# Causal block attention and a mixer block: one written order of 1,507 operations replaced by another

## The chip, the core and the metric

The kernel runs on one core of a Trainium2 chip. The metric is the device time of one execution in microseconds (us), as the median over runs. The core has five engines that work side by side, each through a queue of its own, in order: TensorE (PE; its weight loads are listed apart as PEld), VectorE (DVE), ScalarE (ACT), GpSimd (POOL) and SyncE (SP). POOL's and SP's words here are for the most part issues of DMA transfers. TensorE writes to PSUM, which is cut into banks of 128 x 512 fp32; DVE and ACT read results out of it.

## What is computed

Attention in 8 batches of 8 heads, 576 positions of 64 elements, with a mask of blocks of 64 (a query sees the keys of its own block and of those before it), then a mixer block of two layers on the heads joined to 512 channels:

```python
def _attn_ref(q, k, v):
    B, H, S, D = q.shape                       # 8, 8, 576, 64
    scores = 1.0 / np.sqrt(D) * np.matmul(q, k.transpose(0, 1, 3, 2))
    scores = np.where(block_i >= block_j, scores, -1000000000.0)   # blocks of 64
    attn = np.exp(scores - np.max(scores, axis=-1, keepdims=True))
    attn = attn / (np.sum(attn, axis=-1, keepdims=True) + 1e-09)
    return np.matmul(attn, v).astype(np.float32)

def _moe_ref(x, w_tok1, w_tok2, w_ch1, w_ch2):  # x: heads joined, 8 x 576 x 512
    h = np.maximum(x.transpose(0, 2, 1) @ w_tok1, 0.0) @ w_tok2    # 256 wide
    u = x + h.transpose(0, 2, 1)
    return u + np.maximum(u @ w_ch1, 0.0) @ w_ch2                  # 1536 wide
```

## The kernel before

The program is a list of operations, made once when the kernel is built. Each operation (`P.add`) names the engines that may do it, the operations it depends on, the PSUM banks that it takes and gives back, and a function that emits its instructions. There are 1,509 of them, numbered in the order in which they were added. Their order in time is not worked out when the kernel is built: it is written out in the string `ORDER` (lines 97 to 175), and `Plan.placed` walks it. A word of `ORDER` is a number, an engine letter (T TensorE, A ScalarE, D VectorE, P GpSimd, S SyncE) and, for operations that take PSUM, the letters of the banks: a to d are the four `mm` banks, s and t the two score pairs of the first attention (`sc`), e to h the `late` banks, which stand in the place of s and t once batch 0's scores are done. Each engine's queue holds its own words in that order, and what an operation depends on becomes a wait on a semaphore ahead of it. `ORDER` thus also fixes which engine evacuates a bank and which bank it is.

What runs, stage by stage:

- *Start.* SyncE loads k of the first four heads of batch 0 as fp32 in two halves of 288 KB: rows 0 to 8 are word 13S, rows 9 to 17 word 16S (L426). ScalarE casts them to bf16 (14A and 17A, L395). POOL loads q of those heads in three parts (19P 144 KB, 21P 80 KB, 23P 64 KB, L437), then V (L471), the other heads' k and q, and batch 1's. VectorE transposes each part (15D and 18D for k, 20D, 22D and 24D for q, L442).
- *First attention* (`first_attention`). Score sets (`score_set`, L569) of two heads or four go to the score pairs, and an exponential (`exp`, L587, 128x1024) reads each; there are two pairs, so a third set waits for the first exponential. `tail` copies and clears an edge of the exponentials (L595, L600) on VectorE or POOL. `head_out` (L617) and `ends_out` (L670) multiply with V; a reciprocal and a product on VectorE (L637, L643) make rows of x.
- *Warming matmuls* (`raise_clock`). They multiply zeros: one operation (43) of `WARM` = 11 matmuls of 512 columns (L366) and up to `KEEP` = 37 operations of one matmul of 256 columns (L373; numbers from 44 on). A KEEP word may be left out of `ORDER`; 35 are in it.
- *Later batches.* `attention` makes scores for a batch in six sets of four heads (L569), with exponentials of 128x512 (L776); `token_mix` does the token layer (`token_up` L811 and L815; for batch 0 `first_u`, L871, whose transposes wait for an add on VectorE; u at L910 and L925); `channel_up` (L1038) and its later forms do the first channel layer, `first_down` (L1460) and `channel_down_fast` (L1369, folds at L1393) the second. Where `channel_down_fast` is used, sums and differences of weights and activations stand in for part of the products. The stages of neighbouring batches are woven into each other, so that TensorE has products of one batch while another waits for exponentials.
- *V of the later batches.* `load_v` has five loads per batch (351 to 355 for batch 2; 525 to 529 for batch 3). A load into the buffer of an earlier batch waits for that batch's head outputs.

TensorE works in different tiles of its array: score sets use 32 rows, head outputs and the layers all 128, the row sums of odd pairs another cut. Going from one to another is called a change of tile here.

Of the kernel before, what the change touches and what calls it, by code (L numbers as in the profile page):

```python
# [27 lines left out]
class Plan:  # L28
# [89 lines left out]
    419D 531A 440Tb 97D 414Tc 534A 325Te 533A 98D 326T 532A 415D 437A 416D 542Tahgf 99D 441A 438Tc 545A 327T 439D
    544A 444D 463Tgd 543A 445D 448Thb 328D 466A 464Tc 451D 546A 329S 411Ta 408Te 465A 446D 469T 412D 690P 413D 449Tf
    523D 470A 454T 529P 450A 409D 442Ta 410D 452Tc 455A 443D 691P 467Tg 520D 453A 537Taefh 447D 692P 468A 456T 521D  # L120
    538A 473T 689P 524D 539A 471T 679D 540A 683P 596Ta 457D 541A 474D 562Tcefh 597A 678D 458T 566A 681D 594Ta 565A
    459D 564A 460D 476T 563A 595D 461T 477A 569Tchfe 682D 462A 472D 604Ta 847P 571A 478Tdb 475D 686P 572A 605D 602Tg
    535P 481A 600Th 603D 536P 570A 598Ta 567P 482Tf 601D 607S 568P 553Tc 844P 599D 483A 479Tg 550Th 554D 555D 480A
    488T 551D 484T 552D 606S 489D 486T 485A 556Tc 487D 491T 573A 574Thadg 557D 490D 492A 547Te 558D 577A 493D 497Tbf
    575A 548D 576A 549D 559Tc 578A 688D 701Tedah 498A 685D 579Tg 560D 704A 684D 499T 705A 494D 850P 702A 693P 580D
    585Ta 703A 581D 503T 500D 687D 706Tgdbh 586D 587D 561D 591Te 504D 710A 501Ta 709A 495D 708A 592D 707A 593D 582Tc
    502D 627Tbd 612The 608D 630A 588Tg 583D 496D 505T 859P 615D 858P 633T 584D 506D 507T 857P 634A 589D 590D 860P
    694Tcgab 508D 856P 618T 698A 849D 509T 697A 846D 696A 619D 695A 760Tb 609D 610D 699P 510D 738Tacgh 761A 848D
    631Tf 742A 611D 942P 628Tb 741A 632D 758Th 700P 740A 853P 629D 739A 845D 635T 759A 726Tcbag 636D 723Th 730A 637T
    724D 729A 725D 717Tf 638D 762Th 727A 764Ta 728A 718D 719D 640T 763D 731P 733Tfcbg 641A 732P 765D 768Th 737A 851D  # L130
    766Td 772S 735A 720Ta 769D 711Tg 736A 746Tc 721D 722D 734A 616Th 767D 714Ta 617A 613Tb 712D 773S 713D 642Tdf
    747D 614A 748D 620T 715D 645A 716D 743Tg 622T 621D 639A 648T 744D 511S 745D 646Tb 854D 512S 649A 861Tcagh 338S
    647A 623D 643Td 863A 624D 652T 862A 644D 752Ta 865A 650T 653D 625T 864A 753D 749Tc 754D 626A 655T 866P 852D
    868Tadhg 867P 651D 656A 755Te 871A 770Tf 775D 952P 869A 654D 794Tbh 756D 750D 872A 751D 951P 795Ta 776D 797A
    779Tgc 757D 939P 796D 870A 780Te 782A 800T 657D 798Ta 781A 855D 783Td 771A 785T 799A 784D 948P 809Tef 801A 953P
    802T 777D 812A 778D 787T 803D 945P 786A 804T 815T 788D 789T 805D 816A 905Tbadg 790D 813Te 908A 807T 906A 814D
    792T 808A 810Td 658D 907A 817T 909A 811D 661Tbh 793A 818D 873Tadcg 662D 819T 875A 943D 667T 876A 820D 877A 944D
    874A 822T 941D 893Tdceg 821D 823A 887Ta 659D 897A 884Tf 663T 894A 888D 889D 895A 885D 886D 896A 940D 900Tadcg
    898P 664D 890Tf 904A 899P 881Te 949D 1037P 903A 925Tb 882D 955P 883D 902A 891D 892D 901A 878Te 947D 1040P
    968Tfcdg 926A 950D 954P 922Ta 969A 879D 665Tb 880D 1046P 971A 946D 970A 923D 924D 1043P 972A 956Tedfa 666D 913Tc  # L140
    668D 959A 916Tg 914D 669T 958A 915D 917D 957A 918D 660D 960A 910Td 919Tc 961D 995Tgafe 911D 1052P 920D 921D 670D
    999A 927Tc 1053P 998A 912D 962D 997A 791D 1050P 963Tdbef 996A 671T 928A 1042D 967A 1041D 966A 1000Tacgf 965A
    672D 979Te 964A 1039D 976Tb 1003A 673T 980D 977D 1004A 981D 978D 1002A 988Tbedg 1001A 674D 973Tc 991A 1047D
    1022Tf 676S 990A 974D 975D 989A 1038D 982Ta 992A 985Tc 806D 1054Tdbhe 983D 1023A 984D 993P 1020Tg 1044D 994P
# [1439 lines left out]
```

## Time and profile before

| | us |
|---|---|
| median of 3 runs | 284.48 |
| lowest, highest | 284.04, 285.65 |
| span of the profiled execution | 284.7 |
| TensorE busy | 275.8 |
| VectorE busy | 240.3 |
| ScalarE busy | 180.4 |
| POOL busy | 71.7 |

The profiled execution is one of its own beside the three timed runs; its span, from its first instruction to its last, is what its records give, and no other time of it is known. The views shown below are: the page's busy times and its 40 slices of 7.1 us; busy time of each engine within stretches of the span; the chain of waits, that is, the work that ended last, followed back in time, with start, length, and engine or line; the timeline, with start, length, engine, line, operation, output and input; and the landings of DMA transfers. "issue" in the chain is time in which the engine waited for nothing that the profile shows. Line numbers are those of the kernel before.

### The profile page before, as it was taken

The page shows a single profiled execution, that of the slowest core. Times are in us where ns is not written, and L with a number is a line of the kernel's source. Part 1 is how long each engine was busy: PE and PEld are TensorE (multiplying, and loading weights), DVE is VectorE, ACT ScalarE, POOL GpSimd, SP SyncE. Part 2 cuts the span into 40 slices and gives each one's busy share as a digit, 9 for nine tenths or more (in the row PEclk, how much of TensorE's full clock was granted, in tenths as well). Part 3 has the DMA queues.
Part 4 walks back from the last instruction along what each step waited for, and adds up shares of the span by engine and source line. Part 5 has one row for each costly group of instructions (what it writes and reads, how often), then busy time and mean ns, then how long its engine had stood idle before and what let it go on. Part 6 is the DMA issues. An engine that isn't in the chain of part 4 may idle for free.

```text
span 284.7 us, 9438 instructions
## 1 busy us (share of the span) xinstructions
PE 275.8 (97%) x4038; PEld 197.6 (69%) x4038; DVE 240.3 (84%) x519; ACT 180.4 (63%) x325; POOL 71.7 (25%) x120
## 2 busy tenths in 40 slices
PE   7998999999999899999999999999999999999994
PEld 3667656556878676987777658744488876468883
DVE  3589569799999799999998997997998987598893
ACT  3798685778888358996879785136546653764000
POOL 8975635170641062060341220000000000000000
PEclk9999999999999999999999999999999999999999
DMA  8999999969989495898199587130033403000246
GB/s 160 166 174 202 190 205 203 137 94 134 144 120 119 71 84 87 225 135 122 11 169 102 87 106 132 49 119 18 2 74 98 126 7 131 12 2 0 104 127 212
DMA packets 64776, 31.79 MB, mean 112 GB/s; under 512 B 53088, under 2 KB 55904, under 8 KB 64736
## 3 DMA queue, kind: packets, MB, share of 16 engines
q0 software_dynamic: 45040, 17.64, 53.1%
q1 hardware_dynamic: 19696, 13.57, 19.6%
q8 instruction: 31, 0.51, 0.7%
q14 instruction: 9, 0.07, 0.1%
HBM read 35.85 MB, written 9.44 MB: 159 GB/s over the span
## 4 chain that ended last, share of the span: by engine, by line
PE 92%; DVE 2%; ACT 2%; DMA 1%; issue 1%; SPq 0%; DVEq 0%
PE late L1369 14%; PE mm L1369 11%; PE late L1235 7%; PE mm L1111 7%; PE late L1111 6%; PE mm L569 6%; PE mm L1235 6%; PE mm L617 4%; PE mm L811 3%; PE mm L910 3%; PE mm L1038 3%; PE late L569 2%; PE late L617 2%; PE late L811 2%; PE mm L1460 2%; PE late L1460 2%
## 5 line engine op out<-in xcount | busy, mean ns | idle before, releaser
L776 ACT ACTIVATE e_sb<-late 128x512 bf16<-128x512 f32 x89 | 50.5, 609 | 10.4 <-PE late L569 9.1
L776 ACT ACTIVATE e_sb<-mm 128x512 bf16<-128x512 f32 x79 | 45.1, 609 | 9.9 <-PE late L569 6.6
L471 POOL DMA_DIRECT2D vals<-in_v_dram x45 | 37.2, 844 | 26.7 <-PE late L617 15.9
L442 DVE STREAM_TRANSPOSE qk_sb<-qk_sb 128x288 int32<-128x288 int32 (+2 forms) x57 | 36.2, 694 | 4.6 <-ACT qk_sb L395 3.5
L1369 PEld LDWEIGHTS <-sums 128*128 128x128 bf16 x288 | 27.6, 98 | 5.6 <-issue 1.8
L1369 PEld LDWEIGHTS <-gT 128*128 128x128 bf16 x288 | 27.8, 98 | 4.6
L569 PEld LDWEIGHTS <-qk_sb 32*64 32x64 bf16 x1280 | 19.9, 104 | 13.1 <-issue 8.8
L569 PE MATMUL mm<-qk_sb 32*64 32x64 bf16 (+7 forms) x546 | 27.8, 291 | 0.0
L569 PE MATMUL late<-qk_sb 32*64 32x512 bf16 (+7 forms) x594 | 27.1, 291 | 0.0
L617 PEld LDWEIGHTS <-e_sb 128*128 128x128 bf16 x640 | 23.8, 97 | 4.1 <-issue 0.9
L1111 PEld LDWEIGHTS <-ws_sb 128*128 128x128 bf16 x192 | 17.8, 98 | 3.4 <-issue 1.3
L797 ACT ACTIVATE gT<-mm 128x512 bf16<-128x512 f32 x25 | 14.7, 601 | 7.8 <-PE mm L1111 3.0
L617 PE MATMUL mm<-vals,e_sb 128*128 128x65 bf16 x430 | 19.0, 193 | 0.0
L643 DVE TENSOR_TENSOR x_sb<-mm,rinv 128x256 bf16<-128x256 f32 x43 | 17.9, 421 | 1.1
L1111 PEld LDWEIGHTS <-wc_sb 128*128 128x128 bf16 x144 | 15.4, 114 | 1.8 <-issue 0.2
L1235 PEld LDWEIGHTS <-ws_sb 128*128 128x128 bf16 x96 | 9.3, 98 | 10.1 <-issue 0.2
L1369 PE MATMUL late<-wd_sb,sums 128*128 128x256 bf16 x108 | 13.6, 272 | 1.2 <-issue 1.2
L1369 PE MATMUL late<-wd_sb,gT 128*128 128x256 bf16 x120 | 14.7, 273 | 0.0
L595 POOL COPY vals<-e_sb 128x256 bf16<-128x256 bf16 x10 | 4.1, 412 | 40.9 <-issue 22.9
L395 ACT COPY mm<-late 128x512 f32<-128x512 f32 x17 | 9.9, 584 | 7.1 <-PE late L1235 5.0
L797 ACT ACTIVATE gT<-late 128x512 bf16<-128x512 f32 x17 | 10.2, 602 | 6.3 <-PE late L1235 3.4
L1235 PE MATMUL late<-e_sb,ws_sb 128*128 128x512 bf16 x44 | 12.6, 379 | 0.0
(203 smaller groups left out, 656.2 us busy)
## 6 DMA issues: line engine op xcount, KB each, us to landing
out_dram<-o_sb SPq DMA_DIRECT2D x14, 512.0 KB, 3.1
vals<-in_v_dram POOLq DMA_DIRECT2D x28, 128.0 KB, 5.4
qk_sb<-in_k_dram POOLq DMA_DIRECT2D x12, 288.0 KB, 6.3
qk_sb<-in_q_dram POOLq DMA_DIRECT2D x12, 288.0 KB, 5.9
out_dram<-o_sb SPq DMA_DIRECT2D x7, 256.0 KB, 3.2
wc_sb<-in_moe_w_ch_dram POOLq DMA_DIRECT2D x8, 192.0 KB, 7.7
wc_sb<-in_moe_w_ch_dram POOLq DMA_DIRECT2D x3, 512.0 KB, 10.4
vals<-in_v_dram POOLq DMA_DIRECT2D x15, 64.0 KB, 4.9
```

The costliest lines, as they stand in the source:

```text
L442: nc.vector.transpose(dst[:, 0:S, :] .rearrange("p s e -> p (s e)") .bitcast(I32) .rearrange("p (a k) -> p k a", k=NB)[:, k0:k1], raw2.bit ...
L471: nc.gpsimd.dma_start(out=t[128 - p : 128, J, hs, 0:64], in_=src)
L569: nc.tensor.matmul(out=home(n)[64 * half : 64 * half + 64, c : c + w], lhsT=bar[r, 0] if j is None else kT[i][r, 64 * j : 64 * j + 64, par ...
L617: nc.tensor.matmul(out=u[:, I, 0:65], lhsT=e[:, h, c : c + 128], rhs=vt[:, J, head, 0:65], start=(J == 0), stop=(J == I),)
L643: nc.vector.tensor_tensor(out=xt[:, 0:4, 64 * head : 64 * head + 64], in0=u[:, :, 0:64], in1=ri[:, 0:4].to_broadcast([128, 4, 64]), op=MULT,)
L776: nc.scalar.activation(dst, bank_of(x), EXP, scale=scale)
L797: nc.scalar.activation(dst, src, RELU)
L811: nc.tensor.matmul(out=ps, lhsT=w1_sb[:, c, tt : tt + 255 : 2], rhs=xt[:, c, cols], start=(c == 0), stop=False)
L1111: nc.tensor.matmul(out=bank_of(bank)[:, 256 * o_ : 256 * o_ + 256], lhsT=x(o_, m), rhs=y[:, :, m, :], start=opens, stop=m == 1, skip_group ...
L1235: nc.tensor.matmul(out=bank_of(bank), lhsT=x(m), rhs=y[:, :, m, :], start=first and m == 0, stop=m == 1, skip_group_check=not first,)
L1369: nc.tensor.matmul(out=bank_of(bank)[:, 256 * i : 256 * i + 256], lhsT=x[:, kk, 128 * i : 128 * i + 128], rhs=y[:, kk], start=first and i ...
L1460: nc.tensor.matmul(out=ps, lhsT=gT[0][:, cc, 128 * si : 128 * si + 128], rhs=wc2_sb[:, cc, :], start=cc == 0, stop=cc == NDC - 1,)
```

## The change

Only the string `ORDER` is replaced. It has 76 lines instead of 77, so that every line behind it is numbered one lower in the changed kernel (the score sets are L568 there, head outputs L616). Of the 1,509 operations the old string places 1,507 and the new one 1,485: 22 of the words of KEEP are gone, and 13 are left. All other operations are the same.

What differs beside those: on SyncE 13S goes ahead of 16S. On POOL q's loads are in the order 19P, 21P, 23P instead of 21P, 19P, 23P, and V's loads stand elsewhere. On VectorE the first transposes are 20D, 15D, 22D, 24D, 18D instead of 15D, 20D, 22D, 18D, 24D. TensorE's first score set is 100 instead of 125, and from there on nearly every word has another place. Some evacuations are done by another engine (VectorE's words go from 519 to 522, ScalarE's from 324 to 323, POOL's from 115 to 118, SyncE's from 40 to 35), and five of the last batch's output stores are issued from ScalarE's queue instead of SyncE's. Bank letters differ throughout.

```diff
 ORDER = """
-    16S 0A 11D 10D 13S 9D 21P 1D 2D 43Ta 5D 19P 4D 3D 23P 33P 27P 14A 25P 31P 15D 29P 17A 20D 37P 44Tb 45Tb 46Tb 22D
-    47Ta 36P 48Ta 49Ta 18D 50Ta 51Ta 52Ta 35P 53Ta 24D 54Ta 55Ta 56Ta 125Ts 34P 100Ttbc 179P 126A 28D 57Ta 58Ta 59Ta
-    176P 60Ta 61Ta 26D 62Ta 101A 12P 106Ts 63Ta 32D 182P 64Ta 107A 65Ta 104Tt 42P 30D 66Ta 67Ta 105A 68Ta 39P 123Ts
-    102D 103D 69Ta 70Ta 41P 119A 71Ta 157Tt 124A 112Td 40P 113T 116Ta 108Tb 114D 120A 38P 109T 115D 138Ts 158A 181D
-    81P 72Td 73Tc 74Tc 121D 75Tc 122D 139A 82P 76Tc 7D 144Tt 110D 111D 84P 135Td 178D 127Tc 145A 161Ts 185P 136D
-    117D 137D 140D 131Tb 180D 83P 128T 162A 142Tt 177D 90P 132T 129D 143A 77Td 89P 163Ts 130D 133D 86P 134D 78Td
-    164A 118D 141D 159D 200Tdcba 160D 85P 203A 173Te 154Tf 165Tg 202A 91P 174D 166T 155D 156D 201A 184D 92P 205Tbhfc
-    204A 183D 169Td 88P 170T 209A 167D 263Ta 168D 208A 175D 150Tc 171D 261Tg 172D 207A 187D 267Td 206A 87P 186D
-    146Te 262A 147T 264A 151T 268D 237Tgbfh 152D 339P 6D 148D 269Ta 153D 241A 149D 273Td 189P 240A 270D 281Tc 239A
-    274D 265Te 190P 238A 271Ta 8D 282D 275Tb 266A 191P 193Tdhfg 276A 272D 283Te 196A 277Tc 342P 194A 315Ta 278D
...
-    355P 217D 219Tc 249D 299A 250D 222Th 220D 254Te 221D 363Tdbaf 255D 256D 251Tc 349D 364A 330Te 352P 252D 365A
-    218D 253D 321Td 367A 223D 224D 366A 259D 353P 368Tcghb 420Ta 372A 370A 422Tb 347D 371A 525P 346D 322T 421D 423A
...
-    1465S 1461D 1494T 1464S 1473A 1469D 1476Td 1470D 1478T 1491D 1462T 1479D 1471D 1499D 1482T 1463D 1496Tg 1477D
-    1466S 1483D 1502T 1467S 1497D 1484T 1503D 1500T 1507S 1485D 1495D 1480T 1487S 1501D 1474T 1506S 1481D 1504T
-    1475D 1486S 1505D 1508S
+    11D 4D 1D 9D 13S 0A 19P 10D 14A 16S 5D 3D 20D 15D 17A 21P 22D 23P 24D 43Ta 18D 2D 44Tb 45Tb 46Tb 47Tb 48Tb 49Tb
+    50Tb 51Tb 52Tb 100Tsbc 101A 125Tt 126A 31P 53Td 54Td 55Td 104Ts 106Tt 27P 32D 25P 26D 28D 102D 103D 105A 37P
+    123Ts 107A 29P 30D 119A 120A 35P 121D 124A 122D 33P 36P 34P 116Td 117D 112Ta 113T 114D 179P 181D 176P 108Tb 109T
+    110D 82P 138Tt 111D 139A 40P 157Ts 158A 180D 118D 159D 127Tc 128T 178D 161Tt 162A 115D 182P 144Ts 145A 177D 42P
+    129D 39P 41P 135Td 136D 137D 142Tt 130D 131Ta 132T 133D 134D 143A 163Ts 184D 164A 160D 56Td 200Tdcba 204A 202A
+    205Tefgh 208A 206A 185P 186D 84P 203A 201A 140P 141D 38P 207A 154Ta 155D 81P 165Tc 156D 209A 183D 166T 83P 146Ta
+    147T 167D 168D 90P 150Tg 151T 169Te 170T 148D 152D 92P 173Tb 261Tc 263Td 174D 153D 149D 265Ta 264A 262A 187D
+    237Tghfd 240A 239A 273Tc 266D 86P 238A 269Ta 171D 172D 175D 267Tb 268A 241A 274D 193Techf 194A 270D 12P 271Ta
+    272D 275Tb 276D 196A 8D 277Td 278D 281Te 225Tbagh 282D 197A 226A 228A 85P 279Td 280D 288Tf 283Te 294Tb 284D 87P
+    291Td 88P 292T 293D 89P 227A 229A 232Teagh 235A 7D 234A 233A 289T 339P 341D 230D 231D 295T 296D 340D 91P 303Tg
...
+    301T 242Ta 302D 368Tbgdh 365A 370A 369A 348P 245Tf 349D 371A 243D 345P 246D 247D 330Tc 244D 331T 95P 356Tdbge
+    372A 516P 347D 248Th 249D 350D 251Ta 354P 525P 359A 353P 360A 346D 252D 253D 352P 250D 96D 321Tf 322T 97D 358A
+    357A 361D 355P 388Tdbeg 391A 389A 392A 390A 332T 259D 260D 351P 333D 422Th 518D 423A 513P 519P 400Tagde 404A
...
+    1491D 1460T 1396S 1461D 1479D 1470D 1471D 1498T 1499D 1494T 1462T 1465A 1464A 1497D 1476Tg 1482T 1463D 1477D
+    1467A 1483D 1502T 1503D 1495D 1507A 1466S 1500T 1501D 1506S 1484T 1485D 1487A 1480T 1474T 1504T 1481D 1475D
+    1486S 1505D 1508S
 """
```

More of the change, by code (lines that the diff above doesn't have):

```diff
@@ L118 @@
[L118 to L142, printed above, removed]
@@ new lines @@
+    483A 569Tfdhe 573A 600Tc 570A 479Tb 602Te 601D 606S 488T 572A 486T 460D 480A 574Thcfb 571A 575A 603D 559Td 487D
+    489D 578A 560D 553Ta 576A 554D 555D 604Te 577A 605D 683P 556Th 490D 491T 582Ta 583D 561D 550Tc 551D 557D 558D
+    547Te 492A 588Tg 589D 847P 579Td 585Tf 548D 590D 549D 584D 552D 586D 580D 475A 581D 329S 497Tbh 607S 498A
+    701Taegc 702A 587D 493D 494D 495D 591Td 704A 592D 703A 593D 860P 705A 499T 500D 706Tfega 710A 709A 687D 859P
+    503T 608D 694Tdgac 695A 609D 760Tb 501Td 504D 707A 338S 696A 698A 697A 627Tcg 496D 502D 685D 708A 610D 507T 684D
@@ new lines @@
+    825D 1024Th 1025D 1087A 930D 1030Tf 826D 1095A 937S 1089A 1091P 1254Ta 1066Tdhec 1068A 1031D 1069A 1067A 1070A
+    827D 1252Tb 1253A 1026Tf 1027D 828Teh 829D 1098Tbfcd 1060P 1071Tg 1072D 1073D 830T 1099A 1092P 1103Tg 1104D
+    1105D 1100A 1102A 1112Td 1083Tf 1113D 1114D 1101A 1115Tc 1084D 1085D 1109Tg 1106Td 1034S 1107D 1108D 834T 835D
+    831D 1035S 1137Tbd 1140A 832Tf 833D 1116D 1117D 1255A 1074Te 1110D 1111D 1143T 1075D 1076D 838T 839D 1080Tg
+    1081D 1082D 1077Tc 1197Tae 1118D 1119D 836T 1078D 837D 1079D 840T 1200A 1203T 1141Tf 1204A 1120D 1144D 1138Tc
```

87 lines of the change are left out of this document (50 added, 37 removed).

## The prediction

> **What bounds the kernel now.** I read the page's busy table and slices first, then the chain of waits, then busy time by stretch.
>
> ```profile
> span 284.7 us, 9438 instructions
> PE 275.8 (97%) x4038; PEld 197.6 (69%) x4038; DVE 240.3 (84%) x519; ACT 180.4 (63%) x325; POOL 71.7 (25%) x120
> PE 92%; DVE 2%; ACT 2%; DMA 1%; issue 1%; SPq 0%; DVEq 0%
> 0.00:8.29 8.29, 6.09 (x25) 2.91 (x26) 3.54 (x14) 2.73 (x4) 7.25 (x16) 1.00 0.90 158
> 8.29:20.81 12.52, 12.32 (x299) 8.13 (x298) 8.53 (x29) 11.64 (x14) 10.65 (x19) 1.00 1.49 172
> 20.81:28.43 7.62, 6.87 (x158) 5.61 (x158) 6.89 (x22) 6.60 (x14) 4.17 (x8) 1.00 1.13 201
> 28.43:92.00 63.57, 63.57 (x1140) 42.23 (x1141) 54.88 (x127) 50.06 (x97) 26.93 (x42) 1.00 1.23 149
> 92.00:94.40 2.40, 1.16 (x18) 0.90 (x15) 2.00 (x6) 0.41 (x1) 0.35 (x1) 1.00 1.39 135
> 94.40:147.00 52.60, 52.60 (x978) 42.02 (x978) 48.80 (x109) 41.30 (x78) 16.20 (x27) 1.00 0.79 109
> 147.00:148.50 1.50, 1.19 (x52) 1.01 (x48) 1.47 (x6) 0.33 (x2) 0.66 (x1) 1.00 1.46 197
> 148.50:281.00 132.50, 132.03 (x1386) 94.78 (x1385) 114.18 (x211) 67.30 (x119) 5.53 (x10) 1.00 0.36 78
> ```
>
> In each stretch row the first figure after the colon-pair is the length, then busy PE, PEld, DVE, ACT, POOL. From 28.43 us on TensorE stands still in only two places, at 92 and 147 us. The same products have to be done in either order, so nothing but idle TensorE time, and the work that only fills it, is for sale: the start up to 28.43 us, the two later stops (2.40 - 1.16 = 1.24 and 1.50 - 1.19 = 0.31), and a tail behind the last matmul. Ahead of 20.81 us busy TensorE isn't useful TensorE: it includes the warming matmuls, and ScalarE, busy 11.64 of 12.52 us, sets the pace there with its exponentials.
>
> **First half of k first.** The chain up to the first scores, and the landings of the loads that lead there (size, count, us from issue to landing):
>
> ```profile
> 0.75 0.40 SPq L426
> 1.21 3.96 DMA gT<-in_k_dram
> 5.20 0.68 ACT qk_sb L395
> 5.90 2.35 DVE qk_sb L442 x5
> 8.29 0.63 PE sc L569 x10
> DMA to landing us min/median/max: 2.6/3.3/4.0
> 1.25 1.76 POOL L437 DMA_DIRECT2D qk_sb<-in_q_dram  x3 [0.80 <-POOLq L1568]
> qk_sb<-in_q_dram POOLq DMA_DIRECT2D x3, 144.0 KB, 5.3
> qk_sb<-in_q_dram POOLq DMA_DIRECT2D x1, 80.0 KB, 4.1
> ```
>
> In the old order SyncE issues the second half first; the half that the first cast (14A) waits for is issued at 1.21 and lands at 1.21 + 3.96 = 5.17, though the other was there at 0.75 + 2.6 = 3.35. In the new order the first cast can run at 3.4, and only the second waits until 5.2, so it ends near 5.9. DVE, however, now starts with 20D, the transpose of q's first part. Its load is now POOL's first; the old first load landed at 1.25 + 4.1 = 5.35, and this one is 64 KB longer. At the 0.54 us by which the old second one (144 KB) landed after the first, it lands between 5.35 and 5.9 (an estimate); I take 5.6. Five transposes of 2.35 us in all, the last needing the second cast (5.9), end near 7.95, and the scores start near 8.1 instead of 8.29. What is late next is q, not k. Gain 0.2; bounds: q's load at 5.3 us like the median of its kind gives 6.55 and a loss of 0.6, a load as quick as the 80 KB one gives a gain of 0.6 with the casts next. The move also takes k's second half 0.46 us later through SP's queue; no one reads it before the second cast.
>
> **Half the warming matmuls, and the order of the exponentials.**
>
> ```profile
> 1.66 4.66 PE L366 MATMUL mm<-wd_sb 128*128 128x512 bf16 x11 [1.66 <-DVE wd_sb L340]
> 6.16 1.58 PE L373 MATMUL mm<-wd_sb 128*128 128x256 bf16 x13
> 9.40 0.76 PE mm L373 x6
> 10.74 0.43 PE mm L373 x3
> 8.98 3.84 ACT L587 ACTIVATE e_sb<-sc 128x1024 bf16<-128x1024 f32 x4 [2.54 <-PE sc L569]
> 27.68 0.75 issue
> ```
>
> The eleven long ones stay. Of 35 short ones 13 stay: 9 ahead of the first score (13 before) and 4 behind it (22 before). A short one costs 0.76 / 6 = 0.13, so 18 fewer behind the first score are some 2.3 us of TensorE. I cost their removal at nothing: they lie where TensorE waits for a score buffer, of which there are two, and a buffer comes free when an exponential (3.84 / 4 = 0.96 us each at pace) has read it. If that cover were gone the 2.3 us would be a gain, so that is the upper end; zero is the lower.
>
> What does move the end of this stage is ScalarE: 12.52 - 11.64 = 0.88 us idle there. The new order puts the score sets at equal distances and always two ahead of the exponentials; I follow it by hand and find its last exponential of this stage about 0.5 us earlier besides the 0.2 above. The following stretch idles 0.75 us, the "issue" at 27.68, where 271 (transposes of u) waits for an add on DVE that stands behind others. In the new order other TensorE work (score sets 237 and 193, 225) stands between that add and 271, so I take this stop away whole. By hand the new order has, at about 34 us, six score sets of batch 1 behind it where the old one has four, and eight halves of channel_up instead of seven: some 1.4 us of TensorE work ahead, which agrees with 0.2 + 0.5 + 0.7. Where TensorE is never idle behind, this stays in the end time.
>
> Against fewer warming matmuls speaks the clock: 4.66 / 11 = 0.42 us for one of 512 columns at first, against 0.86 / 4 = 0.215 later (next fence). The Trainium skill, "TensorE: Matmul & The Clock Gate", section "What's actually happening", says that the clock is halved again after an idle window of about 3.4 us. By that rule the 0.8 us that TensorE would stand still ahead of the first score are too short, and the trace agrees as far as it goes: the granted clock stays 1.00 through idles of 0.54 (2.20 less the first 1.66) to 1.24 us. No run here shows a longer one.
>
> **Fewer tile changes.** Ten matmuls of one kind with and without a change of the array's tile ahead of them:
>
> ```profile
> 46.64 0.86 PE late L1460 x4
> 52.70 0.97 PE mm L1460 x4
> ```
>
> A change costs 0.97 - 0.86 = 0.11 us. Counted along TensorE's words there are 122 changes before and 111 after; without the short warming matmuls, whose changes lie under the exponentials, 109 and 106. Three by 0.11 is a gain of 0.3; with all eleven, 1.2.
>
> **The two later stops.** The one at 92 us (1.24) is a score set, 706, that wants a PSUM bank which DVE's fold had not yet read:
>
> ```profile
> 92.08 0.68 DVE L1393 TENSOR_TENSOR o_sb<-mm,u_sb 128x512 f32<-128x512 f32 x1
> 93.13 1.24 issue
> ```
>
> Both stops hang on where single DVE words stand. The new order changes that everywhere. They can go (gain 1.55) or stay (0); nothing in a row says which, so I take half, 0.8.
>
> **New waits.** First the loads of V. 525P, a load of batch 3 that waits for the last head output of batch 1, used to stand behind batch 2's V loads; now 353P, 352P, 355P and 351P, batch 2's, are queued behind it.
>
> ```profile
> 44.93 3.51 POOL L471 DMA_DIRECT2D vals<-in_v_dram  x4 [1.40 <-PE mm L617]
> 50.32 0.87 POOL L471 DMA_DIRECT2D vals<-in_v_dram  x1 [1.89 <-PE mm L815]
> DMA to landing us min/median/max: 5.4/8.5/11.8
> 60.49 0.60 PE mm L617 x20
> ```
>
> Before, the four were issued from 44.93 on (3.51 us), 525 at 50.32, and the first head output of batch 2 ran at 60.49. In the new order that last output of batch 1 ends near 48 us by my count, so the fourth issue of 0.88 is at 51.4, and the first head output of batch 2 (382) stands near 56.3. With the shortest flight of this window, 5.4, it lands at 56.8, 0.5 late; with the median, 8.5, 3.6 late. But the long flights are a queue's length, and here 513P, a load of 288 KB that stood ahead of these, is moved behind them. So I take 0.2, with 0 and 3.6 as bounds.
>
> Second, evacuations that come just in time. With the mean durations of the groups I walked both orders between 32 and 262 us and noted, for each bank that TensorE asks for, how long it had been read: under 0.1 us in 3 of ScalarE's evacuations before, 30 after. At most 30 x 0.1 = 3.0 us are lost; that few fall below zero speaks for less. I take 0.4, bounds 0 and 3.0.
>
> At the end five stores go from SP's queue to ScalarE's; ScalarE is idle then (next rows), and the last fold and its store keep their places: nothing.
>
> ```profile
> 260.00:285.00 25.00, 20.54 (x189) 18.14 (x186) 17.54 (x34) 0.71 (x2) 0.00 (x0) 1.00 0.40 127
> 279.88 0.67 PE late L1369 x6
> 280.57 0.42 DVE o_sb L1393
> ```
>
> **The sum**, against the profiled execution's own 284.7: -0.2 (first scores) -0.5 (exponentials) -0.7 (stop at 27.68) -0.3 (tile changes) -0.8 (later stops) +0.2 (V) +0.4 (just in time) = -1.9, so 282.8. The median of the runs, 284.48, stands 0.2 below the profiled span: 282.6.
>
> **Rivals.**
>
> ```profile
> DMA  8999999969989495898199587130033403000246
> q0 software_dynamic: 45040, 17.64, 53.1%
> DVE  3589569799999799999998997997998987598893
> ```
>
> 1. *V of batch 2 is late* (slower). Place: the first head output of batch 2, behind 525P. It decides once the last of the four takes over 7 us to land. At the median 8.5 TensorE stands 3.6 us instead of 0.2: 282.6 + 3.4 = 286.0. For it: POOL issues strictly in its order, and the DMA slices, 7.1 us each, stand at 8 or 9 up to there; by the share of q0 that is POOL's queue. Against: fewer bytes ahead. Chance 0.15.
> 2. *Tight packing runs over* (slower). The 30 thin margins cost 3.0 rather than 0.4, and DVE, at 9 in most slices between 50 and 150 us, keeps stops as long as the old ones: 282.6 + 2.6 + 0.8 = 286.0. For it: DVE is busy 54.88 of 63.57 us ahead of the stop at 92, so a late word isn't caught up quickly. Against: in the old order only two such margins burst in 250 us. Chance 0.17.
> 3. *The start is hidden anyway* (no change). Up to some 57 us loads follow each other without a gap; if TensorE, being ahead, only meets the weights of the channel layers or V before they land, the 1.4 us go back: 282.6 + 1.4 = 284.0. For it: the slices of DMA. Against: the last stop of the start, at 27.68, is DVE's, and from 28.43 on TensorE waited for no load at all. Chance 0.20.
> 4. *The clock drops.* TensorE would run at half speed until it is released, as in the first 4.66 us, which loses about 2.3: 284.9. Chance 0.03.
>
> The forecast itself has 0.45, between 281.2 and 283.9.
>
> **How the numbers follow.** The measurement tells about 0.5%, 1.4 us, from no change: below 283.06 is faster, above 285.9 slower. Of the forecast's 0.45, 0.37 lie under 283.06 and 0.01 above 285.9; of rival 3's 0.20, 0.04 and 0.01; of the 0.32 of rivals 1 and 2, 0.01 and 0.24, since both can cost more than I priced; of rival 4's 0.03, 0.02 are slower. Faster 0.42, same 0.30, slower 0.28. The range goes from 280.8, where the tile changes bring 1.2 and the later stops 1.55 and nothing new is lost but the 0.4 (282.6 - 0.9 - 0.75 - 0.2 = 280.75), to 286.9, which is the two slower rivals and 0.9 of spread above them; 0.1 is left out at either end.
>
> **What would show it.** Right: first score matmul at 7.9 to 8.2, the last exponential of 128x1024 ending near 20.1, no "issue" near 27, granted clock 1.00. Wrong: a stop ahead of the L616 matmuls near 56 us released by a V load (rival 1); many idles of 0.1 to 0.5 us ahead of TensorE's score sets and products between 32 and 262 us, with DVE or ACT as releaser (rival 2); idles ahead of channel_up near 34 us released by DMA (rival 3).

## The result, and the profile after

| | before | after |
|---|---|---|
| median (lowest, highest), us | 284.26 (283.98 to 285.65), 4 runs | 293.2 (290.84 to 294.91), 4 runs |
| span of the profiled execution | 284.7 | 291.0 |
| its mean granted clock | 1.000 | 0.982 |

The changed kernel is slower: ratio 1.0299, 95% interval 1.0243 to 1.0355. Forecast were 282.6 and a range up to 286.9. Executions more than 1.5% above the fastest of their kernel (three of b_keep32 below, one of the kernel before) are left out of the ratios. A run's time is some 1.8 us above its span, 2.3 at most (292.79 is the time of the execution profiled here, span 291.0; another execution of the old order has 284.06 at a span of 282.3). So the old profile, with its span of 284.7, stands for a run of about 286.5, longer than any of the four in the table, and not for their median.

From the page of the changed kernel: span, busy times, granted clock by slices of 7.3 us, and the queue that carries instructions (transfers, MB, share).

```profile
span 291.0 us, 9353 instructions
PE 275.7 (95%) x3992; PEld 197.6 (68%) x4016; DVE 240.7 (83%) x522; ACT 173.6 (60%) x319; POOL 73.0 (25%) x123
PEclk9957999999999999999999999999999999999999
q8 instruction: 31, 0.51, 0.7%
```

TensorE is as busy as before (275.7 against 275.8) though the 22 warming matmuls are gone (4,016 weight loads instead of 4,038), and the span is 6.3 us longer. The 5 and the 7 among the clock's digits are new; before, all are 9. The stretches of the changed kernel, with the columns of the prediction's table (length; busy PE, PEld, DVE, ACT, POOL; granted clock; DMA):

```profile
8.00:21.86 13.86, 12.39 (x276) 7.84 (x280) 9.05 (x28) 11.59 (x13) 12.41 (x23) 0.74 1.46 175
21.86:35.30 13.44, 13.44 (x327) 10.28 (x312) 9.61 (x27) 10.63 (x23) 7.95 (x12) 0.88 1.31 194
35.30:36.05 0.75, 0.03 (x8) 0.02 (x7) 0.75 (x4) 0.00 (x0) 0.00 (x0) 1.00 2.43 155
36.05:60.59 24.54, 24.35 (x389) 13.87 (x392) 20.84 (x50) 16.92 (x33) 10.37 (x16) 1.00 1.13 144
60.59:61.55 0.96, 0.00 (x0) 0.00 (x1) 0.69 (x1) 0.96 (x3) 0.00 (x0) 1.00 1.16 200
61.55:95.50 33.95, 33.54 (x624) 24.75 (x631) 30.46 (x77) 25.07 (x48) 12.06 (x18) 1.00 1.03 122
95.50:97.10 1.60, 0.35 (x4) 0.07 (x3) 1.53 (x3) 1.60 (x4) 0.78 (x2) 1.00 1.68 166
160.00:163.40 3.40, 2.49 (x80) 1.72 (x78) 1.80 (x5) 2.09 (x5) 0.71 (x2) 1.00 0.21 41
```

Five places stand out: a granted clock of 0.74 and 0.88 up to 35 us, and stops at 35.30, 60.59, 95.50 and 160 to 163 us. The fall of the clock is the fourth rival (chance 0.03), and 60.59 is the place of the first rival. The stop at 95.50 turns out below to be the old one at 92 us, half of which the forecast took away; 35.30 and 160 us are in neither the forecast nor a rival.

**The clock.** In 5 us windows of the changed kernel, then of the one before:

```profile
5.00:10.00 5.00, 3.28 (x73) 2.07 (x75) 3.78 (x9) 1.25 (x2) 4.85 (x9) 1.00 1.47 173
10.00:15.00 5.00, 3.93 (x114) 2.78 (x105) 2.72 (x10) 5.00 (x7) 4.48 (x7) 0.98 1.35 178
15.00:20.00 5.00, 4.85 (x84) 3.32 (x80) 3.58 (x14) 4.14 (x5) 4.53 (x9) 0.50 1.49 176
20.00:25.00 5.00, 5.00 (x96) 2.90 (x89) 3.48 (x12) 3.97 (x8) 2.63 (x7) 0.50 1.17 186
```

```profile
5.00:10.00 5.00, 4.46 (x75) 3.16 (x73) 3.44 (x7) 2.26 (x4) 4.58 (x8) 1.00 1.33 157
10.00:15.00 5.00, 5.00 (x113) 3.21 (x115) 2.44 (x8) 5.00 (x8) 4.92 (x10) 1.00 1.36 174
```

From about 14.8 us on TensorE gets half its clock for 10.2 us. In the 10 us ahead of that it works 3.28 + 3.93 of 10 us; before it is 4.46 + 5.00. What is missing is the warming matmuls, which lie in just those waits.

**The start.** The chain of waits of the changed kernel, and then its exponentials in the timeline (start, length, tiles):

```profile
1.25 4.32 DMA qk_sb<-in_q_dram
5.60 2.34 DVE qk_sb L441 x5
8.00 0.26 PE sc L568 x2
```

```profile
16.99 1.94 ACT L586 ACTIVATE e_sb<-sc 128x1024 bf16<-128x1024 f32 x2 [0.60 <-PE sc L568]
19.16 1.02 ACT L586 ACTIVATE e_sb<-sc 128x1024 bf16<-128x1024 f32 x1 [0.24 <-PE sc L568]
20.84 1.02 ACT L586 ACTIVATE e_sb<-sc 128x1024 bf16<-128x1024 f32 x1 [0.65 <-PE sc L568]
```

The first score stands at 8.00 and waits for q, as forecast (8.1). But the last exponential ends at 21.86, where 20.1 was forecast and 20.75 is the old value: ScalarE now waits for scores that run at half clock.

### The profile page after: what moved, and what is told of

It is laid out like the page before. It is cut to its first block, busy times and chain, and to the rows that moved or that the text cites. A ratio compares the mean times of both kernels' runs of the same rounds, so it can differ in the third digit from the quotient of the medians.

```text
span 291.0 us, 9353 instructions
## 1 busy us (share of the span) xinstructions
PE 275.7 (95%) x3992; PEld 197.6 (68%) x4016; DVE 240.7 (83%) x522; ACT 173.6 (60%) x319; POOL 73.0 (25%) x123
## 4 chain that ended last, share of the span: by engine, by line
PE 86%; DMA 4%; ACT 4%; issue 2%; DVE 2%; POOL 1%; POOLq 0%; ACTq 0%
PE late L1368 16%; PE mm L1368 9%; PE mm L1234 8%; PE late L1110 7%; PE mm L1110 6%; PE late L1234 5%; PE mm L568 4%; PE mm L616 4%; DMA qk_sb<-in_q_dram 4%; PE mm L810 3%; PE late L568 3%; PE late L616 3%; PE mm L1037 2%; ACT e_sb L586 2%; PE late L909 2%
## 5 line engine op out<-in xcount | busy, mean ns | idle before, releaser
L775 ACT ACTIVATE e_sb<-mm 128x512 bf16<-128x512 f32 x86 | 49.1, 614 | 12.5 <-PE mm L568 6.3
L775 ACT ACTIVATE e_sb<-late 128x512 bf16<-128x512 f32 x82 | 47.1, 612 | 7.1 <-PE late L568 4.5
L568 PEld LDWEIGHTS <-qk_sb 32*64 32x64 bf16 x1280 | 20.8, 107 | 14.9 <-issue 10.0
L568 PE MATMUL mm<-qk_sb 32*64 32x64 bf16 (+7 forms) x610 | 28.5, 293 | 0.0
L568 PE MATMUL late<-qk_sb 32*64 32x512 bf16 (+7 forms) x530 | 27.2, 303 | 0.7 <-issue 0.7
L616 PEld LDWEIGHTS <-e_sb 128*128 128x128 bf16 x640 | 23.8, 100 | 5.7 <-issue 2.5
L394 ACT COPY mm<-mm 128x512 f32<-128x512 f32 (+1 forms) x12 | 6.7, 561 | 18.6 <-DVE sums L1350 8.8
L616 PE MATMUL mm<-vals,e_sb 128*128 128x65 bf16 x380 | 17.3, 199 | 0.0
L642 DVE TENSOR_TENSOR x_sb<-mm,rinv 128x256 bf16<-128x256 f32 x38 | 15.8, 419 | 0.8
L1368 PE MATMUL late<-wd_sb,sums 128*128 128x256 bf16 x126 | 15.4, 273 | 0.0
L1368 PE MATMUL late<-wd_sb,gT 128*128 128x256 bf16 x120 | 14.8, 273 | 0.1
L796 ACT ACTIVATE gT<-mm 128x512 bf16<-128x512 f32 x19 | 11.3, 604 | 5.4 <-PE mm L1234 3.1
L1392 DVE TENSOR_TENSOR o_sb<-late,u_sb 128x512 f32<-128x512 f32 x15 | 10.2, 686 | 4.7 <-PE late L1368 4.7
L586 ACT ACTIVATE e_sb<-sc 128x1024 bf16<-128x1024 f32 x11 | 10.8, 1033 | 5.4 <-PE sc L568 5.3
## 6 DMA issues: line engine op xcount, KB each, us to landing
qk_sb<-in_k_dram POOLq DMA_DIRECT2D x12, 288.0 KB, 6.0
qk_sb<-in_q_dram POOLq DMA_DIRECT2D x12, 288.0 KB, 7.3
```

The source lines that it names most:

```text
L394: nc.scalar.copy(dst, src)
L568: nc.tensor.matmul(out=home(n)[64 * half : 64 * half + 64, c : c + w], lhsT=bar[r, 0] if j is None else kT[i][r, 64 * j : 64 * j + 64, par ...
L586: nc.scalar.activation(dst, sc[SC.index(note["pool"])][:, :, 0:n], EXP, scale=scale)
L616: nc.tensor.matmul(out=u[:, I, 0:65], lhsT=e[:, h, c : c + 128], rhs=vt[:, J, head, 0:65], start=(J == 0), stop=(J == I),)
L642: nc.vector.tensor_tensor(out=xt[:, 0:4, 64 * head : 64 * head + 64], in0=u[:, :, 0:64], in1=ri[:, 0:4].to_broadcast([128, 4, 64]), op=MULT,)
L775: nc.scalar.activation(dst, bank_of(x), EXP, scale=scale)
```

## The experiments

Times are medians; the ratio is to the kernel before on the same chip, with its 95% interval. The clock is the mean one of the profiled execution, or of all executions as a span. The warming matmuls feed nothing, so leaving them out or changing them leaves the output as it is. The expectations speak of theories as they stood at the time.

| label | order | us | ratio | clock |
|---|---|---|---|---|
| b_k | old | 284.24 | 0.9988 [0.9974, 1.0003] | 0.998 |
| b_nokeep | old | 288.0 | 1.0119 [1.0094, 1.0145] | 0.973 to 0.975 |
| b_keep11 | old | 285.29 | 1.0027 [1.0003, 1.0051] | 0.994 to 1.000 |
| b_keep32 | old | 285.76 | 0.999 [0.9957, 1.0023] | 0.970 to 1.000 |
| b_k_tr | old | 284.5 | 1.0002 [0.9987, 1.0018] | 1.000 |
| a_keep | new | 292.43 | 1.0275 [1.0232, 1.0317] | 0.990 to 0.996 |
| a_v | new | 292.79 | 1.0274 [1.0238, 1.0311] | 0.973 to 0.997 |
| a_keep_tr | new | 290.27 | 1.0182 [1.0158, 1.0205] | 0.999 |
| a_keep_tr_v_q | new | 288.01 | 1.0106 [1.0072, 1.0141] | 1.000 |
| a_tr_v_q | new | 289.6 | 1.0129 [1.0066, 1.0192] | 0.980 to 0.998 |
| a_all | new | 286.97 | 1.0092 [1.0063, 1.0121] | 1.000 |
| a_all_232 | new | 288.15 | 1.0101 [1.0072, 1.0131] | 1.000 |

### One part of the change alone, in the old order

b_k moves k's first half ahead and nothing else; b_nokeep takes out the same 22 warming matmuls (57 to 78) that the change takes out.

```diff
-    16S 0A 11D 10D 13S 9D 21P
+    13S 0A 11D 10D 16S 9D 21P
```

> The old order with 13S ahead of 16S and nothing else changed. Theory (q's first part is what is late next): first score matmul at 7.8 to 8.0 instead of 8.29, time 0.2 to 0.5 below the old order's. Rival: the new idle time ahead of the scores or q's landing takes it back: same time within 0.2.

The first score comes at 7.89 instead of 8.29 (chain of waits), which the time shows as 0.1%, an interval that holds 1.

```diff
-    ... 57Ta 58Ta 59Ta ... 78Td ...
+    (words 57 to 78 left out)
```

> The old order with the same 22 short warming matmuls (all behind the first score) left out and nothing else changed. Theory 1: the granted clock falls to 0.50 for some 10 us between 12 and 26 us, and the time rises by 2.5 to 4 us, to 286.8 to 288.3. Rival (the clock falls for another reason of the new order): clock 1.00 and a time of 284.3 or up to 1 us less.

The 22 matmuls cost 1.2% when they are gone, 3.1 us beside 284.92 for the kernel before on the same chip. The windows of b_nokeep show why:

```profile
10.00:15.00 5.00, 4.46 (x92) 3.32 (x83) 2.64 (x8) 5.00 (x7) 4.92 (x10) 0.66 1.43 175
15.00:20.00 5.00, 5.00 (x83) 3.08 (x84) 4.12 (x15) 3.12 (x4) 3.56 (x8) 0.50 1.70 176
20.00:25.00 5.00, 4.74 (x103) 3.15 (x95) 2.65 (x12) 4.01 (x6) 3.56 (x7) 0.50 1.12 195
```

The clock falls to 0.50 again, here at 11.6 us and for 13.7 us, with nothing else changed; all four executions have a mean clock of 0.973 to 0.975. So leaving these words out lets the clock fall, in either order. It doesn't force it in the new one: of four executions each, one of a_v and one of a_tr_v_q, both below and both without these words, have 0.997 and 0.998.

### How much warming it takes

b_keep11 leaves out every second of the 22; b_keep32 keeps all, each on 32 rows and 64 columns of the array.

> The old order with every second one of the 22 short warming matmuls behind the first score left out. If the clock's gate has a threshold between no warming and all of it, the mean granted clock shows on which side 11 lie: 1.00 and 284.3 to 285.3, or about 0.974 and 288.

> The old order with the 22 KEEP matmuls behind the first score kept, as long as before (256 columns) but on 32 rows and 64 columns of the array instead of 128 and 128. If the clock's gate counts time with TensorE at work: clock 1.00 and 284.3 to 284.9 as before. If it weighs how much of the array works: the clock falls as without them, and the time is 287 to 288.

```diff
-            def emit(o, bank=bank):
+            def emit(o, bank=bank, n=n):
+                r, c = (32, 64) if n >= 13 else (128, 128)
...
-                    out=bank_of(bank)[:, 0:256], lhsT=zeros[:, 0:128], rhs=zeros[:, 0:256],
+                    out=bank_of(bank)[0:c, 0:256], lhsT=zeros[0:r, 0:c], rhs=zeros[0:r, 0:256],
```

With eleven, no execution of eight falls below 0.994. With 22 small ones, three of ten executions have a clock of 0.970 to 0.973 and take 288.59 to 291.22 us, the other seven 0.997 to 1.000 and 283.73 to 286.8. Of 54 executions of the kernel before, one has such a clock (0.976, 289.76 us). That hints at an edge, and that it counts how much of the array works and not only that it works; ten executions don't settle it, and where an edge lies was not measured.

### The warming matmuls put back into the new order

```diff
-    ... 104Ts 106Tt 27P ... 123Ts 107A ... 138Tt 111D ... 157Ts 158A ... 161Tt 162A ... 144Ts 145A ... 142Tt 130D
+    ... 104Ts 57Ta 58Ta 59Ta 106Tt 60Ta 61Ta 62Ta 63Ta 64Ta 65Ta 27P ... 123Ts 66Ta 67Ta 68Ta 107A ...
+    138Tt 69Tc 70Tc 71Tc 111D ... 157Ts 72Tc 73Tc 158A ... 161Tt 74Tb 75Tb 162A ... 144Ts 76Tb 145A ... 142Tt 77Tb 78Tb 130D
```

> The new order with the 22 left-out short warming matmuls put back among the first attention's score sets. Theory 1 (too few warming matmuls let the clock fall at 14.9 us, and that costs the most): granted clock 1.00 throughout, the last exponential of 128x1024 ends near 20 us, and the time falls from 293.2 by the 2.5 us by which the new order is behind at 26 us and some 1 us that it should be ahead there: 289.7 (288.5 to 290.7). Rival (the clock is a side show, since ScalarE sets the pace there, and the loss is made later): clock 1.00, but not under 292.

At the start the clock stays, but 292.43 and 1.0275 are hardly less than the change itself. In the new order as it stands the start is therefore not most of the loss. The same stop near 95 us is in a_keep too, and longer. Its chain of waits, and then its windows:

```profile
92.83 1.82 issue
94.65 0.50 PE mm L670 x19
```

```profile
92.00:94.00 2.00, 0.83 (x34) 0.53 (x33) 1.93 (x6) 1.79 (x4) 0.00 (x0) 1.00 1.14 99
94.00:96.00 2.00, 1.35 (x27) 1.18 (x28) 1.93 (x4) 0.85 (x2) 0.00 (x0) 0.95 1.11 341
96.00:98.00 2.00, 2.00 (x22) 0.73 (x20) 0.83 (x3) 0.00 (x0) 1.59 (x2) 0.50 0.91 288
```

Here it takes the clock down: to 0.50 from 95.8 us on, for 3.4 us.

### What the stops at 92 to 97 us are

In the chain the stop is "issue": nothing that the profile shows releases it. TensorE's weight loads in the timeline of the kernel before, then of the changed one, with the idle time ahead in brackets:

```profile
94.37 0.31 PEld L1369 LDWEIGHTS <-sums 128*128 128x128 bf16 x3 [1.42 <-issue]
```

```profile
97.08 0.88 PEld L1368 LDWEIGHTS <-gT 128*128 128x128 bf16 x9 [1.53 <-issue]
```

Different words (sums, gT) in different orders. But counted from the start (in the windows, the x behind PEld), up to the stop of before, of after and of a_keep:

```profile
0.00:93.50 93.50, 89.98 (x1630) 59.75 (x1631) 75.29 (x194) 71.44 (x128) 49.34 (x83) 1.00 1.23 156
```

```profile
0.00:96.30 96.30, 89.08 (x1621) 59.06 (x1631) 75.62 (x197) 68.80 (x123) 49.66 (x83) 0.95 1.17 152
```

```profile
0.00:93.80 93.80, 88.85 (x1621) 58.43 (x1631) 75.26 (x197) 68.62 (x123) 49.72 (x83) 1.00 1.19 150
```

Three times 1631 weight loads, whatever stands there. The stops at 27.68 us before (479 loads) and 35.30 after (608) fit the same ladder: 1631 - 479 = 9 x 128, 608 - 479 = 128 and one. So does a further stop of the changed kernel, 0.71 us from 159.05 on, just ahead of the one at 160 (2783 - 1631 = 9 x 128):

```profile
0.00:159.30 159.30, 150.65 (x2765) 107.80 (x2783) 133.75 (x323) 119.69 (x221) 68.24 (x114) 0.97 1.04 137
```

A stop that hangs on the number of instructions, not on which they are, is read here as the next block of TensorE's own instructions coming late. The queue q8 on the page carries instructions, 31 transfers in all, 0.51 / 31 MB = 16 KB each. By their records one starts at 92.02 before and at 94.47 after, and TensorE goes on 2.35 and 2.6 us later. The table of DMA queues of the changed kernel between 84.1 and 94.4 us has no row of q8, but these:

```profile
q0 software_dynamic: 3166, 1.24, 109.1%
q1 hardware_dynamic: 935, 0.24, 21.9%
uT<-u_sb SPq DMA_TRANSPOSE x2, 8.2
```

From 94.4 to 97.1 it has one:

```profile
q8 instruction: 1, 0.02, 2.7%
```

So for ten microseconds no transfer of instructions starts, while the DMA engines serve SyncE's two transposes 606S and 607S (the first of the program) and POOL's loads beside them. Before, the first transpose is issued at 83.42, the fetch starts 8.60 us later, and the transpose lands after 10.6; after, it is 87.57, 6.90 and 9.1; in a_keep 85.33, 6.75 and 9.2. The fetch needs 2.4 to 2.6 us, so the block comes within 0.4 us of the transpose's landing; in a_v, which has this stop too (1.49 us), it comes 1.9 us behind it. Whether the transpose holds it or the loads hold both isn't told apart here. But a late block needs no transpose: ahead of the stops at 35.30 and 159.05 us none is under way, and beside the one row of q8 the DMA tables (29.9 to 36.05 us, 155.9 to 159.7) have only q0, POOL's loads. TensorE gets to the block's end 7.3 to 7.9 us after the first transpose in the new order, 9.4 in the old.

The Trainium skill, "Runtime: NRT & Kernel Launch", section "Instruction fetch mechanics", says that instructions are refilled in blocks of 16 KiB while the current block runs, and that crossing a block is mostly hidden. The size agrees with the 16 KB here. That it is hidden doesn't hold where other transfers are dense: 0.4 us (at load 608 in a_all) to 1.8 (in a_keep) stand open at one block.

### The loads beside the transposes moved away

In a_keep_tr 844P and 847P, loads of a later batch's k and q, go behind 859P; 848D, which reads one of them, moves with them.

```diff
-    ... 844P 482Ta ... 847P 579Td ... 859P 503T ... 634D 848D 631Te ... 510D 849D
+    ... 482Ta ... 579Td ... 859P 844P 847P 503T ... 634D 631Te ... 510D 848D 849D
```

> a_keep with the loads 844P and 847P (k and q of batch 5) moved behind 859P, and 848D next to 849D, so that no POOL load of theirs is in flight when SyncE's first two DMA transposes (606S, 607S) are. Theory 2 (TensorE's stop at 92 to 98 us is a late fetch of its own instructions: the transposes and the loads hold the DMA rings until 6.8 us after 606S, the fetch of the block that begins at weight load 1631 starts only then and takes 2.4 us): the fetch starts earlier, the stop of 2.0 us before weight load 1631 shrinks below 0.5, the clock stays 1.00 there, and the time falls from 292.4 by 2 to 3.5 us, to 289 to 290.4. Rival (a product there waits for a bank that VectorE reads late): the stop stays, and the time is 292.4 within 0.6.

A clear gain: 1.0275 to 1.0182. The chain of a_keep_tr at the place of the stop, and the landing of its first transpose:

```profile
93.32 0.44 PE mm L670 x20
93.75 1.42 PE mm L1369 x12
```

```profile
uT<-u_sb SPq DMA_TRANSPOSE x1, 3.8
```

No "issue" between them, and the transpose lands in 3.8 us instead of 9.2 in a_keep. The fetch starts at 89.08, before the block runs out, and the clock stays 1.00. So that stop goes with the loads beside the transposes, although TensorE's own words are the same: its cause is shown as far as the loads, not how they delay the fetch.

In the old order the same was tried (b_k_tr: 844P and 847P behind 693P, with b_k's edit).

> The old order with 13S ahead of 16S and the loads 847P and 844P moved behind 693P, away from the two DMA transposes 606S and 607S. Theory 2: the fetch for weight load 1631 is never late, the stop at 92 us, which some executions of the old order have, never comes: time 0.4 to 1.5 us below the old order and faster than both kernels. Rival: same as the old order with 13S ahead of 16S, 0.0 to 0.4 us below the old one.

The first transpose lands in 5.3 us instead of 8.7 in b_k and the fetch starts earlier (86.23 against 88.84), but the time is that of b_k: there the block is in time anyway, in the execution profiled of b_k too. The profiled executions of b_keep11 and b_keep32 have no stop over 0.5 us at that load either. The stop at 92 in the old profile is thus taken as one of that execution and not of the usual one, and what the forecast took from it was not for sale.

### V of batch 2, and q and k of batch 7

a_v sends 525P behind 351P, as the first rival suggests.

```diff
-    ... 251Ta 354P 525P 359A ... 260D 351P 333D
+    ... 251Ta 354P 359A ... 260D 351P 525P 333D
```

> The new order with 525P moved behind 353P, 352P, 355P and 351P. Theory: the 0.96 us stop ahead of the first head output of batch 2 (382) is gone, time 292.2 (291.7 to 292.7). Rival (the V loads land no earlier, or another load is late then): 293.2 within 0.4.

What the stop at 60.59 is: POOL's timeline of the changed kernel, then what the weight loads wait for behind 36 us.

```profile
52.40 0.88 POOL L470 DMA_DIRECT2D vals<-in_v_dram  x1 [6.76 <-PE mm L616]
53.89 3.32 POOL L470 DMA_DIRECT2D vals<-in_v_dram  x4 [0.61 <-issue]
```

```profile
PEld L616 <- DMA vals<-in_v_dram: 1.3, 1, 1.3
```

POOL stands 6.76 us at 525P, and the head output behind waits for V. In a_v it starts at once (chain of a_v):

```profile
61.06 0.05 issue
61.11 0.47 PE late L616 x10
```

The rival's mechanism is right, its price is 0.96 us and not 3.6, since the fourth load lands 5.2 us after its issue. Taken away by itself it brings no measurable time (1.0274 against 1.0299): TensorE being earlier only waits longer at the next stop.

That next one is at 160 to 163 us. POOL's timeline of the changed kernel, then VectorE's:

```profile
151.36 0.40 POOL L594 COPY vals<-e_sb 128x256 bf16<-128x256 bf16 x1 [6.37 <-ACT e_sb L775]
154.46 0.56 POOL L418 DMA_DIRECT2D qk_sb<-in_q_dram  x1
```

```profile
160.86 0.72 DVE L441 STREAM_TRANSPOSE qk_sb<-qk_sb 128x288 int32<-128x288 int32 x1 [1.13 <-DMA qk_sb<-in_k_dram]
162.27 0.72 DVE L441 STREAM_TRANSPOSE qk_sb<-qk_sb 128x288 int32<-128x288 int32 x1 [0.68 <-DMA qk_sb<-in_q_dram]
```

The loads of q and k of batch 7 (1043P, 1046P) stand on POOL behind a copy, 961P, that waits 6.37 us for an exponential. They land at 160.8 and 162.2, VectorE waits for them in its order, and the products behind VectorE wait with it. a_keep_tr_v_q puts both loads ahead of the copies, besides a_v's edit.

```diff
-    ... 950D 913Td ... 958A 959A 961P 915D 962P 916Td ... 947D 911D ... 1053P 1043P 918D ... 974D 1046P 976Te
+    ... 950D 1046P 913Td ... 958A 959A 915D 916Td ... 947D 1043P 961P 962P 911D ... 1053P 918D ... 974D 976Te
```

> a_keep_tr with two more moves on POOL: 525P behind 351P (V of batch 2 first), and the loads 1046P and 1043P (q and k of batch 7's second half) ahead of the tail copy 961P that waits for exponentials. Theory 3 (the stop at 160 us is VectorE standing at transposes whose loads were issued too late): the stops at 382 and 935 go, 0.4 and 1.7 us, and the time is 1.5 to 2.5 us below a_keep_tr: about 287.5. Rival (each stop removed comes back at the next late transfer): within 0.7 of a_keep_tr.

1.0182 goes to 1.0106. The times don't tell the two edits apart; a_v's alone brought nothing while the others stood. The traces do: in a_keep_tr TensorE stands still 0.63 us for V (from 59.31) and 1.85 us behind the transpose of q (from 158.69). In a_keep_tr_v_q both are gone: it works 10.00 of 10 us from 55 on and 15.00 of 15 from 150 on, against 9.37 and 13.15.

### The same without the warming matmuls, and what is left

a_tr_v_q is a_keep_tr_v_q without the 22 words again.

> a_keep_tr_v_q without the 22 put-back warming matmuls: the new order as it was, but for the three moves of transfers. Theory 1 (the clock's fall in the first attention costs the new order what it costs the old one, 3 us, once the later waits no longer absorb it): clock 0.97 to 0.98, time 2.3 to 3.3 us above a_keep_tr_v_q: 290.3 to 291.3. Rival (the new order loses little to the clock, as a_keep showed only 0.8 us): under 289.3.

289.6 against 288.01, between what the theory and its rival said; the intervals of the two ratios overlap. Within this one kernel three executions have a clock of 0.980 or 0.981 and take 289.43 to 290.03 us, one has 0.998 and takes 287.25: 2.2 to 2.8 us between them, at equal words. In a_v, where the later stops stand, it is 1.5 to 1.7 (291.21 at 0.997; 292.68 to 292.93 at the others). So this is about the price of the clock once the later stops no longer hide part of it, from one execution on the one side.

a_all is a_keep_tr_v_q with the five output stores back in SyncE's queue (1464, 1465, 1467, 1487, 1507).

```diff
-    ... 1465A 1464A ... 1467A ... 1507A ... 1487A ...
+    ... 1465S 1464S ... 1467S ... 1507S ... 1487S ...
```

> a_keep_tr_v_q with the five stores at the end that the new order issues from ScalarE's queue (1464, 1465, 1467, 1487, 1507) issued from SyncE's again. Theory 4 (in the new order the span ends 4.9 us after TensorE's last matmul and in the old one 4.2, because of these stores): the end after the last matmul comes back to 4.2 to 4.4, time 0.4 to 0.8 below a_keep_tr_v_q: about 287.4. Rival (the longer end is that of the stores' places, not of the queue): same within 0.3.

1.0092 against 1.0106, inside the intervals. The end, by the chains of a_all and then of b_k:

```profile
279.72 0.42 DVE o_sb L1393
```

```profile
278.33 0.42 DVE o_sb L1393
```

The spans are 284.7 and 282.5: 4.98 us from the last fold's start to the end in a_all, 4.17 in b_k. The end stays 0.8 longer with the stores on either queue, so the queue of these five is not the cause. In front of it 1.4 us are left.

a_all_232 tries the start once more: 289T and 295T ahead of 232.

```diff
-    ... 229A 232Teagh 235A 7D 234A 233A 289T 339P 341D 230D 231D 295T 296D
+    ... 229A 289T 295T 232Teagh 235A 7D 234A 233A 339P 341D 230D 231D 296D
```

> a_all with two halves of channel_up (289T, 295T) moved ahead of the score set 232, in which TensorE runs out of instructions at weight load 608 near 33 us. Theory 2: the same block is reached 0.4 to 0.9 us later with useful work done meanwhile, the stop of 0.8 to 1.1 us there goes or halves, time 286.0 to 286.6. Rival (ScalarE's exponentials of 232 are then late for the next scores, or the fetch starts later as well): 287.0 within 0.4.

Not a gain (1.0101). The fetch for load 608 is late here too, 0.63 us in the chain (from 33.65), against 0.41 in a_all. Behind it TensorE waits another 0.76 us (from 35.67), of which the chain gives 0.59 to one of ScalarE's exponentials: the rival's mechanism.

No version beats the kernel before beyond its interval; b_k, at 0.9988, is the nearest.

## Why the prediction was wrong, step by step

By the ratios, and in the order in which things were put right, the loss of 2.99% goes: warming matmuls 0.24, late fetch near 95 us 0.93, V with q and k of batch 7 0.76, stores 0.14 (the first and the last not beyond their intervals), left 0.92. In another order of repair the shares would differ; the warming matmuls alone are 1.2% in the old order.

- *First scores, -0.2.* Right in mechanism and size: 8.00 instead of 8.29, q last. Not visible in the time, even by itself (b_k).
- *Half the warming matmuls, costed at nothing.* This step failed, and with it the chance of 0.03 for the fourth rival. "They lie where TensorE waits for a score buffer" is true; that what lies in a wait is free is not. They hold the clock, and b_nokeep prices them at 3.1 us in the old order. The argument from the clock counted single idles: the longest here is that ahead of the first score, the 1.46 us of the second fence below. What counts in their place stays open. It isn't TensorE's busy share over 10 us alone: by the next two rows the clock fell behind 8.60 of 10 us (a_tr_v_q, at 13.9) and stayed through 8.15 (a_keep_tr).

```profile
3.90:13.90 10.00, 8.60 (x150) 4.86 (x152) 5.31 (x13) 6.07 (x9) 9.80 (x16) 1.00 1.35 167
150.60:160.60 10.00, 8.15 (x198) 5.95 (x198) 7.90 (x18) 8.76 (x18) 2.89 (x7) 1.00 0.84 126
```

  The Trainium skill, "TensorE: Matmul & The Clock Gate", section "What's actually happening", has the clock halved after an idle window of about 3.4 us. By that rule, read as one unbroken idle, it would have stayed; the traces don't agree, as the clock fell after 3.28 and 3.93 us of work in two windows of 5 us. This row is from TensorE's timeline in the changed kernel:

```profile
7.99 0.33 PE L568 MATMUL sc<-qk_sb 32*64 32x320 bf16 x2 [1.46 <-DVE bar L339]
```

- *Exponentials, -0.5.* Failed. At 21.86 they end 1.1 later than before, because half-clock scores come late. That isn't all: in a_keep, with the clock whole, the last one ends at 21.16, still not earlier than 20.75. ScalarE waits 0.43 and 0.18 us for scores there, and only 0.15 in the old order, where the forecast had the scores always two sets ahead.
- *The stop at 27.68, -0.7.* The cause was wrong. It was put down to an add on VectorE and said to go with the order. It is at load 479, and in the new order the next block's, at load 608, takes its place with 0.75 us. The chain said "issue", that is, no releaser; a releaser was read into it from the words that stood near.
- *Half of the later stops, -0.8.* The same error at 92 us, where VectorE's fold was named. The new order brings 606S closer ahead of the block's end and the stop stays: 1.24 us in the chain before, 1.25 after and 1.82 in a_keep, with a fall of the clock behind it there. The small one at 147 us the chain does give to VectorE (a product from 147.96 to 148.39); no run here singles it out.
- *Fewer tile changes, -0.3.* Nothing in these runs shows it or refutes it. The two rows that it rests on are of four matmuls each, not ten.
- *V, +0.2.* Right mechanism, 0.96 us; the term was too small, but well below its bound of 3.6.
- *Just in time, +0.4.* No row of small stops behind VectorE or ScalarE: in the 24.54 and 33.95 us around the V stop TensorE idles 0.19 and 0.41 us, and from 163.4 to 262 us it is busy 98.29 of 98.60. The second rival did not come.
- *The tail at nothing.* 4.98 us (in a_all) against 4.17 behind the last fold. Its cause is open.
- *Not in the prediction at all:* the fetch of TensorE's own instructions, and loads of batch 7 that were moved behind a waiting copy on POOL. It names the rule (what is queued behind a word that waits) for 525P and didn't walk the rest of POOL's queue by it.

The baseline added an error too: the sum was made against a span that had a stop of 1.24 us which the four other profiled executions of the old order with the clock whole (b_k, b_k_tr, b_keep11, b_keep32, each with a small edit) haven't got.

Open stay the 0.9% of a_all (of it 0.8 us at the end and 1.4 ahead of it, in which the fetch at load 608 has 0.41), and what the clock asks for.

## What to carry to other kernels

Filler work in a wait is not free to remove: leave it out alone in one run and read the granted clock there before costing it at nothing. A stop that the chain calls "issue" has no releaser; count instructions up to it in two orders before naming one, and look at what the DMA queues carry while the next block of instructions should come. When an order is rewritten, walk each DMA queue for every load that now stands behind a word that waits, since putting one right only lengthens the wait at the next.

## What was not expected of the hardware

- The granted clock fell to 0.50 behind no idle of TensorE above 1.5 us from its first matmul on. It stayed there for 10.24 us (changed kernel, a_v, a_tr_v_q) or 13.65 (b_nokeep), and for 3.41 behind the 1.82 us stop of a_keep: three, four and one times 3.41. Eleven matmuls of 256 columns among the waits hold it (0.994 and above), 22 on 32 rows held it in seven executions of ten.
- A late block of TensorE's instructions stands open by 0.4 to 1.8 us in the chain; 128 weight loads lie between two blocks in this kernel.
- The first DMA transpose takes 9.2 us to land with three of POOL's loads issued ahead of it (a_keep) and 3.8 with two of them moved away (a_keep_tr), and the fetch of the next block of instructions, in the same stretch, comes within 0.4 us of the transpose's landing in three of the four profiled executions that have this stop.
